# Bilinear attention and projection on one core: two engines copy, and two queues store, each finished sum of the state rows

## The chip, the core and the metric

The kernel runs on one core of a Trainium2 chip. The metric is the device time of one execution in microseconds, lower is better; before the change it is 489.55 us, the median of 3 runs (488.55 to 490.4).

## What is computed

```python
def _attn_ref(x, state):                       # x (8, 8, 512, 64), state (8, 8, 32, 64)
    scores = scale * np.matmul(x, state.transpose(0, 1, 3, 2))
    a = softmax(scores)
    xread = np.matmul(a, state)                # 512 token rows of a batch and head
    scores2 = scale * np.matmul(state, x.transpose(0, 1, 3, 2))
    a2 = softmax(scores2)
    sread = np.matmul(a2, x)                   # 32 state rows of a batch and head
    return np.concatenate([xread, sread], axis=2)

def _moe_ref(x, w1, w2, w3, w_out):            # x: (8 * 544, 512), the heads side by side
    a = x @ w1
    b = x @ w2
    h = a * b @ w3
    return h @ w_out                           # (8 * 544, 512)
```

(`softmax` stands for the four lines that subtract the maximum, take exp and divide by the sum.) The last step is, for each row, `((x w1) * (x w2)) @ (w3 w_out)`. The output has, for each of 8 batches, 512 token rows and behind them 32 state rows, each of 512 float32 numbers (2 KB).

## The kernel before

Weights are converted first, and `w3 w_out` is multiplied out once into `wo` (a high and a low part of each number). The token rows of the 8 batches follow, batch by batch. The read-outs of the state rows of all batches are collected in `sread`, and only when the last batch is done does `state_rows` (L741) turn them into output rows: 8 batches of 32 state rows are 256 rows, `n = B * NS`. It is the last part of the program, and nothing comes behind it.

`state_rows` first makes, for each of 8 blocks `ft` of 128 hidden columns, the product of the two projections, a high and a low part (`gs`). Then it makes the output rows in two groups `tt` of 128 rows (L766): group 0 holds the state rows of batches 0 to 3, group 1 those of batches 4 to 7. A group is one call of `stage2` (L362). It takes a bank of PSUM (`bank`, one of two buffers of 128 x 512 float32, tile `ps_o`), adds up 8 x 3 matmuls of 512 columns in it (`project`, L355), and calls `store` (L368). There ScalarE copies the 512 columns from PSUM into a tile `tmp` in SBUF in one instruction (L371), and four transfers (L373) write 32 rows each, one for each batch:

```python
for (dest, first, n), queue in zip(dests, cycle((nc.scalar, nc.sync))):
    queue.dma_start(out=dest, in_=o[first:first + n])
```

So the transfers go in turn to ScalarE's queue and to SyncE's queue, two on each, 64 KB each: 32 rows of 2 KB that lie one behind the other in SBUF's partitions and in the output.

The order of TensorE's and SyncE's instructions is that of the program text; ScalarE's and VectorE's is set by a scheduler, which a `high_priority` block moves ahead of other ready work. The waits between engines are put in by the framework, from the tiles that instructions read and write.

The token rows of batches 1 to 7 are stored in another way, which the prediction uses for comparison: `stored_quarter` (L497, transfers at L500) writes 128 rows of 256 columns in one transfer from ScalarE's queue, 128 KB in runs of 1 KB.

Of the kernel before, what the change touches and what calls it, by code (L numbers as in the profile page):

```python
# [22 lines left out]
F32 = mybir.dt.float32  # L23
# [6 lines left out]
P = 128  # L30
NF = 512
# [9 lines left out]
def attn_bilinear_kernel(  # L41
# [10 lines left out]
    nc = tc.nc  # L52
    B, _, NT, H, D = x_s.shape
    S = NT * P
    NP = H // 2
    NS = st.shape[3]
    KT = H * NS // P
    FT, DO = w34_k.shape[0], out.shape[2]
# [3 lines left out]
    PER = P // NS  # L62
# [6 lines left out]
    main = ctx.enter_context(tc.tile_pool(name="main", bufs=2))  # L69
# [20 lines left out]
    def bank():  # L90
        return ps_o.tile([P, NF], F32, name="ps_o")

    def two_banks():
        return ps_2.tile([P, 2, NF], F32, name="ps_2")

    def split(hi, lo, src):

        return (
            nc.scalar.copy(out=hi, in_=src),  # L99
            nc.vector.tensor_tensor(out=lo, in0=src, in1=hi.bitcast(F32), op=ALU.subtract),  # L100
        )
# [227 lines left out]
    def new_g(ft):  # L329
        if ft < FT - 2:  # L330
            return [main.tile([P, NF], F32R, name=f"g_{part}", bufs=FT - 2) for part in ("hi", "lo")]
        both = main.tile([P, 2, NF], F32R, name="g_x", bufs=2)
        return [both[:, 0], both[:, 1]]
# [21 lines left out]
    def project(ps, gs, tt, ft):  # L355
        g_hi, g_lo = (g[:, tt * P:(tt + 1) * P] for g in gs[ft])
        for k, (g, w) in enumerate(((g_hi, "lo"), (g_hi, "hi"), (g_lo, "hi"))):
            nc.tensor.matmul(  # L358
                ps[:, :DO], g, wo[w][:, ft, :], start=(ft == 0 and k == 0), stop=(ft == FT - 1 and k == 2)
            )  # L360

    def stage2(gs, tt, dests):  # L362
        ps = bank()
        for ft in range(FT):
            project(ps, gs, tt, ft)
        store(ps, dests)

    def store(ps, dests):  # L368
        o = main.tile([P, NF], F32, name="tmp", bufs=4)[:, :DO]
        with tc.high_priority():  # L370
            stored[:] = [nc.scalar.copy(out=o, in_=ps[:, :DO])]  # L371
        for (dest, first, n), queue in zip(dests, cycle((nc.scalar, nc.sync))):
            queue.dma_start(out=dest, in_=o[first:first + n])  # L373
# [20 lines left out]
    HT, HO = S // 2, DO // 2  # L394
# [253 lines left out]
    gs, acc, early = [], [], range(2)  # L648
# [92 lines left out]
    def state_rows():  # L741
        n = B * NS

        sr = att.tile([P, NP, 2, n], F32R, name="x_d", bufs=1)
        split(sr[:, :, 1], sr[:, :, 0], sread)
        gs = []
        for ft in range(FT):
            quarter, c = divmod(ft * P, NQ)
            ps = two_banks()
            for i in range(2):  # L750
                wh, wl = (main.tile([P, NP * P], F32R, name=f"sw_{part}", bufs=2 * HALF) for part in ("hi", "lo"))
                as_w = lambda t: t.rearrange("p (j f) -> p j f", j=NP)
                split(as_w(wh), as_w(wl), w_sb[:, quarter, i, :, c:c + P])
                rows = [slice(kt * P, (kt + 1) * P) for kt in range(NP)]
                for kt, ks in enumerate(rows):
                    nc.tensor.matmul(ps[:, i], wh[:, ks], sr[:, kt], start=(kt == 0), stop=False)  # L756
                for kt, ks in enumerate(rows):
                    nc.tensor.matmul(ps[:, i, :n], wl[:, ks], sr[:, kt, 1], start=False, stop=(kt == NP - 1))  # L758
            sums = main.tile([P, 2, n], F32, name="tmp", bufs=4)
            halves = ps.rearrange("p i (half n) -> p i half n", n=n)  # L760
            nc.scalar.copy(out=sums, in_=halves[:, :, 1])
            nc.vector.tensor_tensor(out=sums, in0=sums, in1=halves[:, :, 0], op=ALU.add)
            nc.vector.tensor_tensor(out=sums[:, 0], in0=sums[:, 0], in1=sums[:, 1], op=ALU.mult)
            gs.append([g[:, :n] for g in new_g(ft)])
            split(*gs[-1], sums[:, 0])
        for tt in range(n // P):  # L766
            stage2(gs, tt, [(out[tt * PER + q, S:], q * NS, NS) for q in range(PER)])


    for b in range(PLAIN, B):  # L770
# [1 line left out]
    with tc.issue_after(last_split[0].ins), tc.issue_after(last_split[1].ins):  # L772
        state_rows()
# [44 lines left out]
```

## Time and profile before

| what | value |
|---|---|
| runs | 488.55, 489.55, 490.4 us, median 489.55 |
| span of the profiled execution, first to last instruction | 486.2 us |
| time of the profiled execution outside its span | not recorded; the median is 3.35 us above the span |
| TensorE busy (matmuls) | 479.5 us, 99% of the span |
| VectorE, ScalarE busy | 393.4 us (81%), 237.6 us (49%) |
| granted TensorE clock | 1.000 of full speed, the mean of the core |
| stores of the state rows and of batch 0's token rows | 12 transfers at L373 |

The span is the time from the first to the last instruction that the profiler saw. A share of the span is an average over all stages. What happens at the very end of the program is read from the timeline, where an instruction stands with its start and its duration, and from the table of DMA windows, where the mean busy share of the core's 16 DMA engines stands with the rate that they moved. The time from a transfer's issue to its landing is counted from the start of the issuing instruction to the last of its completions.

### The profile page before, as it was taken

Reading aid. Unit: us, or ns where it says so; the run is one execution under the profiler, and the core shown is the slowest. Engines: PE = TensorE matmul, PEld = TensorE weight load, DVE = VectorE, ACT = ScalarE, POOL = GpSimd, SP = SyncE. Lnnn points to the kernel's source line nnn. Section 1 sums busy time; section 2 is a strip of 40 time slices with the busy share of each in tenths; the row PEclk is TensorE's granted clock in tenths of the full one; section 3 lists DMA queues with packets and bytes.
Section 4 is the critical chain, followed back from the end, with each engine's and each line's share of the span. In section 5 each row is a group of like instructions: output and inputs, shape, how many; then the busy total and the mean of one; then the engine's idle time right before and its main releaser. Section 6 shows DMA issues by size and latency. Waiting matters only on the chain.

```text
span 486.2 us, 8627 instructions
## 1 busy us (share of the span) xinstructions
PE 479.5 (99%) x3398; PEld 370.2 (76%) x3398; DVE 393.4 (81%) x580; ACT 237.6 (49%) x368; POOL 0.2 (0%) x4
## 2 busy tenths in 40 slices
PE   8999999999999999999999999999999999999996
PEld 5554467768788878887797779777977797899885
DVE  5778999798899589959985998599859985678870
ACT  4876984453547045605560555055515642353640
POOL 0000000000000000000000000000000000000000
PEclk9999999999999999999999999999999999999999
DMA  8996971163014404130413042304230223001101
GB/s 345 367 399 222 388 278 26 19 216 89 14 38 173 106 4 182 38 93 4 182 41 92 5 181 45 87 5 181 47 84 6 89 47 85 5 2 45 45 1 43
DMA packets 56361, 52.49 MB, mean 108 GB/s; under 512 B 42752, under 2 KB 50944, under 8 KB 51712
## 3 DMA queue, kind: packets, MB, share of 16 engines
q1 hardware_dynamic: 47488, 43.27, 26.8%
q10 hardware_dynamic: 8832, 8.65, 5.2%
q8 instruction: 27, 0.44, 0.4%
q14 instruction: 14, 0.11, 0.1%
HBM read 38.27 MB, written 8.91 MB: 97 GB/s over the span
## 4 chain that ended last, share of the span: by engine, by line
PE 93%; DVE 4%; ACT 1%; DMA 1%; issue 0%; DVEq 0%; ACTq 0%
PE ps L344 36%; PE ps_o L460 11%; PE ps L472 8%; PE ps L151 8%; PE ps_o L358 7%; PE ps_o L465 6%; PE ps L477 4%; PE ps L756 3%; PE ps_o L615 2%; PE ps L615 2%; PE ps_o L635 2%; PE ps L758 2%; PE ps_o L276 1%; DVE w_sb L138 1%; DMA raw<-in_w_k_dram 1%; PE ps L612 1%
## 5 line engine op out<-in xcount | busy, mean ns | idle before, releaser
L344 PE MATMUL ps<-at_lo,sw_hi 128*128 128x512 f32 x256 | 101.1, 395 | 0.0
L344 PE MATMUL ps<-at_hi,sw_hi 128*128 128x512 f32 x256 | 99.7, 389 | 0.0
L344 PE MATMUL ps<-at_hi,sw_lo 128*128 128x512 f32 x256 | 99.7, 389 | 0.0
L549 ACT COPY tmp<-ps 128x512 f32<-128x512 f32 x56 | 32.8, 585 | 121.5 <-PE ps L344 119.3
L344 PEld LDWEIGHTS ps<-at_lo,sw_hi 128*128 128x128 f32 x256 | 48.1, 188 | 15.9 <-DVE g_lo L100 4.2
L344 PEld LDWEIGHTS ps<-at_hi,sw_lo 128*128 128x128 f32 x256 | 48.1, 188 | 10.3
L344 PEld LDWEIGHTS ps<-at_hi,sw_hi 128*128 128x128 f32 x256 | 48.1, 188 | 9.5 <-issue 0.2
L488 DVE TENSOR_TENSOR tmp<-tmp,ps 128x512 f32<-128x512 f32 x42 | 28.9, 688 | 19.0 <-PE ps L477 18.1
L429 DVE TENSOR_TENSOR g_x<-tmp,ps 128x512 f32<-128x512 f32 x28 | 19.0, 679 | 26.4 <-ACT tmp L549 26.3
L100 DVE TENSOR_TENSOR sw_lo<-ps,sw_hi 128x1024 fp32r<-128x1024 f32 (+1 forms) x34 | 38.2, 1149 | 1.3 <-ACT sw_hi L99 1.3
L99 ACT CAST g_hi<-raw 128x512 fp32r<-128x512 f32 x42 | 24.6, 619 | 29.1 <-DVE raw L429 21.6
L151 PE MATMUL ps<-w_sb,st 64*32 64x512 f32 (+1 forms) x544 | 31.6, 570 | 0.4 <-DVE sw_lo L100 0.4
L99 ACT CAST sw_hi<-ps 128x1024 fp32r<-128x1024 f32 (+1 forms) x34 | 31.1, 969 | 1.8 <-PE ps L151 1.7
L460 PEld LDWEIGHTS ps_o<-t,g_hi 128*128 128x128 f32 x224 | 27.8, 191 | 5.0 <-issue 5.0
L99 ACT CAST g_hi<-g_x 128x512 fp32r<-128x512 f32 x42 | 25.6, 625 | 10.3 <-DVE g_x L429 5.3
L460 PE MATMUL ps_o<-t,g_hi 128*128 128x256 f32 x224 | 29.7, 286 | 0.0
L100 DVE TENSOR_TENSOR g_lo<-raw,g_hi 128x512 fp32r<-128x512 f32 x42 | 28.0, 681 | 1.6 <-PE ps_o L465 1.6
L460 PE MATMUL ps_o<-wo,g_hi 128*128 128x256 f32 x224 | 29.1, 283 | 0.0
L460 PEld LDWEIGHTS ps_o<-wo,g_hi 128*128 128x128 f32 x224 | 28.3, 192 | 0.5
L100 DVE TENSOR_TENSOR g_lo<-g_x,g_hi 128x512 fp32r<-128x512 f32 x42 | 27.2, 684 | 1.8 <-PE ps_o L465 1.8
L472 PE MATMUL ps<-t,g_hi 128*128 128x512 f32 x112 | 28.0, 392 | 0.0
L472 PEld LDWEIGHTS ps<-t,g_hi 128*128 128x128 f32 x112 | 20.2, 189 | 3.6
(125 smaller groups left out, 802.6 us busy)
## 6 DMA issues: line engine op xcount, KB each, us to landing
raw<-in_w_k_dram SPq DMA_DIRECT2D x8, 1024.0 KB, 6.0
x_d<-in_x_d_dram SPq DMA_DIRECT2D x8, 1024.0 KB, 7.4
raw<-in_w_dram SPq DMA_DIRECT2D x8, 1024.0 KB, 6.6
x_s<-in_x_s_dram SPq DMA_DIRECT2D x8, 1024.0 KB, 5.1
out_dram<-tmp ACTq DMA_DIRECT2D x56, 128.0 KB, 1.8
raw<-in_w3t_dram SPq DMA_DIRECT2D x4, 1024.0 KB, 7.0
e<-work SPq DMA_DIRECT2D x112, 32.0 KB, 2.0
sread<-turned SPq DMA_DIRECT2D x128, 4.0 KB, 1.7
```

Source lines behind the costliest of these rows:

```text
L99: nc.scalar.copy(out=hi, in_=src),
L100: nc.vector.tensor_tensor(out=lo, in0=src, in1=hi.bitcast(F32), op=ALU.subtract),
L151: nc.tensor.matmul(ps[j * NS:(j + 1) * NS, q], sts[b][rows, j], moving(rows, j), start=True, stop=True)
L344: nc.tensor.matmul(ps[:, i], w[:, kt, c:c + P], a[:, kt], start=(k == 0), stop=(k == 3 * KT - 1))
L358: nc.tensor.matmul(ps[:, :DO], g, wo[w][:, ft, :], start=(ft == 0 and k == 0), stop=(ft == FT - 1 and k == 2))
L460: nc.tensor.matmul(ps[:, tt * HO:(tt + 1) * HO], g, w(part, k), start=(fresh and k == 0 and tt == 0 and part == "lo"), stop=False, skip_gr ...
L465: nc.tensor.matmul(ps[:, tt * HO:(tt + 1) * HO], g, w("hi", k), start=False, stop=(k == QF - 1), skip_group_check=True)
L472: nc.tensor.matmul(ps[:, tt].rearrange("p (n d) -> p n d", n=2), g, w(k), start=(k == 0), stop=False, skip_group_check=True,)
L477: nc.tensor.matmul(ps[:, tt, :HO], g, w(k)[:, 0], start=False, stop=(k == QF - 1), skip_group_check=True)
L488: sum2 = lambda out, x, y: nc.vector.tensor_tensor(out=out, in0=x, in1=y, op=ALU.add)
L549: copied = nc.scalar.copy(out=a_sb, in_=ps[:, 0])
L615: nc.tensor.matmul(w34_ps[i][:, :DO], chunks[k][:, DO + i * P:DO + (i + 1) * P], w_out[k], start=(k == 0), stop=(k == FT - 1),)
```

## The change

The two calls of `stage2` in `state_rows` are written out in place. Each group's sum is now copied out of PSUM by two instructions, the first 256 columns by ScalarE and the last 256 by VectorE (`HO` is 256), and each half is stored by one transfer of 128 rows by 256 columns (128 KB): ScalarE's half on ScalarE's queue, VectorE's half on SyncE's queue. The destination is the 4 batches' slices of the output at once, 4 x 32 rows. All other calls of `store` stay.

```diff
         for tt in range(n // P):
-            stage2(gs, tt, [(out[tt * PER + q, S:], q * NS, NS) for q in range(PER)])
+            dest = out[tt * PER:(tt + 1) * PER, S:]
+            ps = bank()
+            for ft in range(FT):
+                project(ps, gs, tt, ft)
+            o = main.tile([P, NF], F32, name="tmp", bufs=4)
+            for k, (copy, queue) in enumerate(((nc.scalar.copy, nc.scalar), (nc.vector.tensor_copy, nc.sync))):
+                cols = slice(k * HO, (k + 1) * HO)
+                with tc.high_priority():
+                    copy(out=o[:, cols], in_=ps[:, cols])
+                queue.dma_start(out=dest[:, :, cols], in_=o[:, cols])
```

How the built program's instructions stand now, with the engines that each waits for in brackets (a name such as `PE_49` is the semaphore that TensorE counts up when an instruction ends). TensorE's instructions are the same as before. On ScalarE, at the end of the program (`-` before, `+` now; `tmp` is the tile in SBUF, `ps_o` the bank of PSUM, sizes are those of what is written):

```order
 L761 COPY tmp<-ps_4850 128x512 [waits PE_49,Activation_49]
 L99 CAST g_x<-tmp 128x256 [waits DVE_49]
-L371 COPY tmp<-ps_o 128x512 [waits PE_49,Activation_49]
-L373 DMA out_dram<-tmp 32x512 [waits Activation_49]
-L373 DMA out_dram<-tmp 32x512
-L371 COPY tmp<-ps_o 128x512 [waits PE_49]
-L373 DMA out_dram<-tmp 32x512 [waits Activation_49]
-L373 DMA out_dram<-tmp 32x512
-L814 UNCONDITIONAL_BRANCH
+L775 COPY tmp<-ps_o 128x256 [waits PE_49,Activation_49]
+L776 DMA out_dram<-tmp 4x32x256 [waits Activation_49]
+L775 COPY tmp<-ps_o 128x256 [waits PE_49]
```

ScalarE's copy still waits for TensorE and is half as wide; behind it stands one transfer instead of two, whose destination is written as 4 x 32 x 256 numbers.

On VectorE, at the end of the program:

```order
 L763 TENSOR_TENSOR tmp<-tmp 128x256 [waits DVE_49]
 L100 TENSOR_TENSOR g_x<-tmp,g_x 128x256 [waits Activation_49]
-L814 UNCONDITIONAL_BRANCH
+L775 COPY tmp<-ps_o 128x256 [waits Activation_49] x2
+L823 UNCONDITIONAL_BRANCH
```

The two new copies stand behind all other work of VectorE. Each waits for ScalarE (`Activation_49`), and not for TensorE.

On SyncE, at the end of the program:

```order
 L175 DMA sread<-turned 32x32 [waits DMAHW6_49]
 L175 DMA sread<-turned 32x32 [waits DMAHW7_49]
-L373 DMA out_dram<-tmp 32x512 [waits DMAHW1_49,Activation_49]
-L373 DMA out_dram<-tmp 32x512 [waits DMAHW3_49]
-L373 DMA out_dram<-tmp 32x512 [waits DMAHW5_49,Activation_49]
-L373 DMA out_dram<-tmp 32x512 [waits DMAHW7_49]
-L814 UNCONDITIONAL_BRANCH
+L776 DMA out_dram<-tmp 4x32x256 [waits DMAHW1_49,DVE_49]
+L776 DMA out_dram<-tmp 4x32x256 [waits DMAHW3_49,DVE_49]
```

SyncE issues two transfers where there were four, and each waits for VectorE's copy instead of ScalarE's.

## Rows read from the trace of the kernel before

**Rows 1.** The page: busy time, share of the span and number of instructions of each engine.

```profile
PE 479.5 (99%) x3398; PEld 370.2 (76%) x3398; DVE 393.4 (81%) x580; ACT 237.6 (49%) x368; POOL 0.2 (0%) x4
```

**Rows 2.** The chain of work that ended last, in order of time, from 470 us to the end: start, duration, what.

```profile
471.36 10.93 PE ps_o L358 x48
482.29 0.02 issue
482.31 0.59 ACT tmp L371
```

**Rows 3.** The timeline from 482.3 us to the end of the span: start, duration, engine (ACTq and SPq are issues of DMAs), line, what, in brackets the idle time before it and what ended it.

```profile
482.31 0.59 ACT L371 COPY tmp<-ps_o 128x512 f32<-128x512 f32 x1 [4.80 <-PE ps_o L358]
482.92 0.78 SPq L373 DMA_DIRECT2D out_dram<-tmp  x2
482.92 0.85 ACTq L373 DMA_DIRECT2D out_dram<-tmp  x2
```

**Rows 4.** DMA issues between 483.2 and 483.4 us, the last of the program: number, KB each, us from issue to landing; and the issues of L373 from 476 us on, with duration in ns (least, median, most), first and last start.

```profile
out_dram<-tmp SPq DMA_DIRECT2D x1, 64.0 KB, 1.6
out_dram<-tmp ACTq DMA_DIRECT2D x1, 64.0 KB, 1.9
...
L373 SPq DMA_DIRECT2D out_dram<-tmp x4: 314/393/421, 477.5 to 483.3; - x4
L373 ACTq DMA_DIRECT2D out_dram<-tmp x4: 374/412/444, 477.5 to 483.3; - x4
```

**Rows 5.** Windows of the last 3 us: from, to, length, busy time of PE, PEld, DVE, ACT and POOL with numbers of instructions, granted clock, mean busy share of the 16 DMA engines, GB/s.

```profile
483.40:483.60 0.20, 0.00 (x0) 0.00 (x0) 0.00 (x0) 0.00 (x0) 0.00 (x0) 1.00 0.00 0
483.60:483.80 0.20, 0.00 (x0) 0.00 (x0) 0.00 (x0) 0.00 (x0) 0.00 (x0) 1.00 0.33 82
...
484.00:484.20 0.20, 0.00 (x0) 0.00 (x0) 0.00 (x0) 0.00 (x0) 0.00 (x0) 1.00 0.79 195
...
484.60:484.80 0.20, 0.00 (x0) 0.00 (x0) 0.00 (x0) 0.00 (x0) 0.00 (x0) 1.00 0.91 215
484.80:485.00 0.20, 0.00 (x0) 0.00 (x0) 0.00 (x0) 0.00 (x0) 0.00 (x0) 1.00 0.10 21
485.00:485.20 0.20, 0.00 (x0) 0.00 (x0) 0.00 (x0) 0.00 (x0) 0.00 (x0) 1.00 0.00 0
```

**Rows 6.** Groups of instructions by line and shape, ScalarE: busy time, mean ns of one, idle time before and what ended it.

```profile
L371 ACT COPY tmp<-ps_o 128x512 f32<-128x512 f32 x6 | 3.5, 588 | 13.6 <-PE ps_o L358 13.6
...
L99 ACT CAST g_hi<-tmp 128x512 fp32r<-128x512 f32 x20 | 12.4, 618 | 3.4 <-DVE tmp L326 3.2
...
L99 ACT CAST g_hi<-tmp 128x256 fp32r<-128x256 f32 x6 | 2.4, 402 | 1.4 <-DVE tmp L763 1.4
```

**Rows 7.** The same view, VectorE: an operation on 512 columns that reads PSUM (`ps`), one on 128 columns that reads PSUM (`ps_o`), one on 256 columns in SBUF, and one with a single source in SBUF.

```profile
L762 DVE TENSOR_TENSOR tmp<-tmp,ps 128x512 f32<-128x512 f32 x8 | 5.5, 683 | 2.5 <-ACT tmp L761 2.5
...
L763 DVE TENSOR_TENSOR tmp<-tmp 128x256 f32<-128x256 f32 x8 | 3.4, 422 | 0.1
...
L281 DVE TENSOR_TENSOR scaled<-ps_o,sum 128x128 f32<-128x128 f32 x7 | 2.0, 284 | 0.0
...
L134 DVE TENSOR_SCALAR w_sb<-w_sb 128x512 int32<-128x512 int32 x2 | 0.8, 418 | 0.0
```

**Rows 8.** The timeline at 452 us: a VectorE instruction that waits for a ScalarE copy out of PSUM.

```profile
452.12 0.59 ACT L761 COPY tmp<-ps 128x512 f32<-128x512 f32 x1 [1.54 <-PE ps L758]
...
452.74 0.69 DVE L762 TENSOR_TENSOR tmp<-tmp,ps 128x512 f32<-128x512 f32 x1 [1.44 <-ACT tmp L761]
```

**Rows 9.** The transposes at L196 and the exponentials at L209, which both read the same PSUM tile `ps`, with duration in ns; and who waited for whom (us in total, times, longest).

```profile
L196 DVE STREAM_TRANSPOSE work<-ps x8: 1242/1243/1251, 39.9 to 369.0; 128x1024 f32<-128x1024 f32 x8
...
L209 ACT ACTIVATE e<-ps,m x16: 679/688/701, 42.6 to 371.0; 128x512 f32<-128x512 f32 x16
...
ACT e L209 <- DVE work L196: 7.5, 6, 1.9
```

**Rows 10.** A pair of 128 KB stores of token rows (L500, 128 rows by 256 columns each): the issues in the timeline, their times to landing, and windows with the columns of rows 5.

```profile
438.28 0.83 ACTq L500 DMA_DIRECT2D out_dram<-tmp  x2
...
out_dram<-tmp ACTq DMA_DIRECT2D x2, 128.0 KB, 1.8
...
438.30:439.10 0.80, 0.80 (x9) 0.80 (x8) 0.25 (x1) 0.00 (x0) 0.00 (x0) 1.00 0.00 0
439.10:439.30 0.20, 0.20 (x4) 0.20 (x3) 0.00 (x0) 0.10 (x1) 0.00 (x0) 1.00 0.71 256
439.30:439.50 0.20, 0.20 (x4) 0.20 (x3) 0.00 (x0) 0.20 (x1) 0.00 (x0) 1.00 1.03 359
...
439.90:440.10 0.20, 0.20 (x4) 0.20 (x3) 0.00 (x0) 0.20 (x1) 0.00 (x0) 1.00 0.63 210
440.10:440.30 0.20, 0.20 (x4) 0.20 (x3) 0.17 (x1) 0.20 (x2) 0.00 (x0) 1.00 0.00 0
```

**Rows 11.** Group 0, stored while group 1 is multiplied: its copy in the timeline, and windows from its issue to the end of the matmuls.

```profile
476.92 0.59 ACT L371 COPY tmp<-ps_o 128x512 f32<-128x512 f32 x1 [3.27 <-PE ps_o L358]
...
478.30:479.60 1.30, 1.30 (x7) 1.09 (x6) 0.00 (x0) 0.00 (x0) 0.00 (x0) 1.00 0.79 202
479.60:482.30 2.70, 2.67 (x12) 1.88 (x10) 0.00 (x0) 0.00 (x0) 0.00 (x0) 1.00 0.00 0
```

## Prediction, made before the changed kernel was run

> **What bounds the kernel now.** The page comes first: TensorE is busy 99% of the span [rows 1], so nothing that other engines do beside it counts, unless it makes TensorE wait. The chain of waits says where TensorE stops being the bound: its last run of matmuls ends at 482.29 us, and then one copy by ScalarE is on the path [rows 2]. The timeline of the end [rows 3] and the DMA views [rows 4, 5] show the rest, which I call the tail. The copy runs from 482.31 to 482.90. At 482.92 both queues begin to issue two transfers each; the second ones start at 483.3, and the last of these lands 1.9 us later, at 485.2 to 485.3. The DMA engines are idle until about 483.7, busy until about 484.9, and the landing comes 0.4 us after they fall idle. From there to the end of the span at 486.2 there are 0.9 us in which the engines close the program. So from the last matmul to the last landing there are 3.0 us, 0.6% of the time. That is all that this change can act on at the end.
>
> **The span and the runs.** The profiled execution has a span of 486.2 us; the runs have a median of 489.55 us, 3.35 us more. I make the sum for the tail of the span and add the difference to 489.55. A measurement of this kernel can tell about 0.5% from no change, 2.45 us: faster is below 487.1, slower is above 492.0.
>
> **Group 0 costs nothing.** Its copy starts at 476.92, and its transfers ran under group 1's matmuls: the DMA engines are idle again from 479.6 to 482.3 [rows 11]. The new copies stand behind all other work of VectorE, and the two groups use the two buffers of `ps_o`, so no matmul waits for them. If group 0's transfers kept the DMA engines busy for 3.2 us instead of 1.3, they would end at about 481.5, before group 1's are issued at 482.7. The cover is group 1's matmuls; without it, group 0 would cost what group 1 does. On ScalarE the copy of group 1 stands behind one transfer of group 0 instead of two, and it waits for TensorE until 482.29 anyway.
>
> **The copies of group 1.** ScalarE's copy of 512 columns takes 0.59 us. A cast of 256 columns is 216 ns shorter than one of 512 (618 against 402) [rows 6]; taken off, the half copy needs 0.38 us: from 482.31 to 482.69, and its transfer is issued at 482.71. VectorE's copy does not run at once with it. In the built program it waits for ScalarE, not for TensorE, and the only work of ScalarE that it can be waiting for is the other half's copy, out of the same bank. The trace shows the same between two other readers of one PSUM tile: the exponentials read `ps` and a small tile, and waited 7.5 us in all for transposes that read `ps` [rows 9]. So the copies go one behind the other, with 0.03 us between them, as where VectorE follows ScalarE at 452.74 [rows 8]. No row has a VectorE copy out of PSUM. By 683 ns for 512 and 284 ns for 128 columns from PSUM it would be 284 + 128 x 1.04 = 417 ns, and 422 ns is that of 256 columns with two sources in SBUF; the operation with one source needs 418 ns for 512 columns, so perhaps 0.2 to 0.3 us for 256 [rows 7]. I take 0.42 us, because the first row reads PSUM as this copy does. It ends at 483.14, and SyncE issues at 483.16. Against the second issues before, at 483.3, the last issue is only 0.15 us earlier.
>
> **The transfers of group 1.** Before, 4 x 64 KB were moved, now 2 x 128 KB, the same 256 KB. What differs is the shape. The stores of token rows are written as 128 x 256 and land 1.8 us after their issue; in their windows all 16 DMA engines are busy (a share of 1.03) at 359 GB/s, 22.4 GB/s for each, 45.6 ns for a run of 1 KB [rows 10]. The old stores had 32 rows in front and came to a share of 0.91 [rows 5]. Both counts in front divide by 16. The new destination is written as 4 x 32 x 256, with 4 in front. No row shows what the hardware makes of a 4. The bounds are these: all 16 engines share the work, as at L500, or four of them do all of it, one for each of the four slices.
>
> With 16 engines the later transfer lands 1.8 us after 483.16, at 484.96, 0.34 us before 485.3.
>
> With four engines, and the same four for both queues, each has 256 KB / 4 = 64 runs of 1 KB to move. They begin 0.82 us after the first issue, as at L500 (issued at 438.28, idle until 439.10 [rows 10]), at 483.53. SyncE's transfer comes 0.45 us later, while ScalarE's 32 runs still need 1.46 us, so the four engines don't fall idle. They need 64 x 45.6 ns = 2.92 us, until 486.45, and with 0.4 us to the landing it is 486.85: 1.55 us later than before. In this case the order of the copies no longer matters: the engines start after ScalarE's half and work without a gap.
>
> I take four. The count in front is the one thing in which these transfers differ from those at L500, which have the same rows, columns and bytes, and for ScalarE's half the same queue; the rows show full shares only where that count is a multiple of 16. This is an inference, and the weight of the other bound is below. The Trainium skill has a rule for it (DMA: Bandwidth & Descriptors, "Why a DMA increments its semaphore by 16 and not by 1"): the number of engines of a transfer is the largest number up to 16 that divides the slowest dimension of both sides, and for these queues it is the lowest-numbered ones. By it, 4 and 128 would give four engines, the same for both queues, and the sum +1.55 us; if all 16 took part, it would be -0.34 us. No run here shows the rule at work for a small count.
>
> **The sum.** Copies and issues -0.15 us, transfers +1.7 us: **+1.55 us, 489.55 + 1.55 = 491.1 us**, a span of about 487.7.
>
> **The rivals.**
> - *All 16 engines.* The DMA spreads 4 x 32 rows as it spreads 128. For it: every store in the trace has a share near 1 [rows 5, 10]. Against it: the count of 4. It gives 489.55 - 0.34 = 489.2 us.
> - *The copies really run at once, and 16 engines.* Both halves are issued at 482.71 and land 1.8 to 1.9 us later, at 484.6: -0.7 us, 488.85 us. Against it stand VectorE's wait and the rows of two readers of one tile [rows 9]. Even a tail that stored in no time at all after the copy would not reach 0.5%: 485.3 - 2.45 is 482.85, before the copy of today ends.
> - *Four engines that are slower than at L500.* Here the place is each of the four engines, where the runs of two queues meet. In the tail the two queues also overlapped, and at 484.0 the engines made 195 GB/s at a share of 0.79 [rows 5]: 15.4 GB/s for a busy engine, 66.4 ns for 1 KB. Then 64 runs need 4.25 us, until 487.78, the landing is at 488.18: +2.9 us, 492.4 us, slower by 0.6%. It decides from 60 ns a run on, for then 64 runs need 3.82 us and the loss is 2.45. Against it: later in the same tail the share was 0.91 at 215 GB/s, so the rate of 195 is partly one of engines that had just begun.
>
> **How the numbers follow.** Four engines at L500's rate: 0.62. All 16 engines with the copies in turn: 0.22. Copies at once with 16 engines: 0.03. Four slow engines: 0.13. The last alone is slower by over 0.5%; the runs scatter by 0.9 us to each side of the median, and 0.02 of the first case is put on that side for it: slower 0.15. No case is faster by over 0.5%, and 0.01 is left for scatter. Within 0.5%: 0.84. The likeliest time is 491.1 us, by itself with 490.2 to 492.0 by the scatter. The range of 8 in 10 reaches down to the cases with 16 engines and up to the slow four: 488.7 to 492.5 us.
>
> **What would show it.** In the profile after, the matmuls should end at about 482.3 and the half copy on ScalarE take 0.38 us. VectorE's copy should start some 0.03 us behind ScalarE's end and take 0.3 to 0.42 us. Right about the transfers: in the windows behind the last matmul the DMA share stands near 0.25, at about 90 GB/s, for some 2.9 us, and issue to landing is 3 us or more. A share near 1 for 0.8 us, with landings after 1.8 us, would make the four engines wrong and give 489.2. If VectorE's copy starts with ScalarE's, the wait was misread. A share of 0.25 at 60 GB/s would be the slow case. If the span before 482 moves by over 1 us, something else changed that I don't see.

## The result, and the profile after

The changed kernel takes 491.87 us (median of 6 runs, 490.85 to 492.74), the one before 489.53 us (median of 6, 488.55 to 490.4). The ratio is 1.0055, with a 95% interval of 1.0039 to 1.0072: slower, by about what a measurement of this kernel can tell. The forecast was 491.1 us in a range of 488.7 to 492.5, for the case that four DMA engines do all of the last store. The profile shows that case, with a tail somewhat longer than forecast.

By *tail* I mean here the time from the end of the last matmul to the end of the span. Before, it was 486.2 - 482.29 = 3.9 us [rows 2]. After, the page and the chain of waits from 470 us on (start, duration, what) say:

```profile
span 489.6 us, 8624 instructions
...
PE 480.0 (98%) x3398; PEld 370.4 (76%) x3398; DVE 394.2 (81%) x582; ACT 237.2 (48%) x368; POOL 0.2 (0%) x4
```

```profile
472.52 10.93 PE ps_o L358 x48
483.45 0.02 issue
483.47 0.38 ACT tmp L775
483.85 0.02 issue
483.87 0.42 DVE tmp L775
```

The last run of matmuls has the same 48 instructions and the same 10.93 us as in [rows 2], and ends at 483.45. The tail is 489.6 - 483.45 = 6.2 us, 2.3 us more than before. (Spans are printed rounded to 0.1 us; tails are worked out from the unrounded spans, here 489.63 and 486.17, so the last digit can differ by one.) The chain now has two copies in a row where it had one. The timeline of the tail, to set beside [rows 3]:

```profile
483.47 0.37 ACT L775 COPY tmp<-ps_o 128x256 f32<-128x256 f32 x1 [5.01 <-PE ps_o L358]
483.87 0.55 ACTq L776 DMA_DIRECT2D out_dram<-tmp  x1
483.87 0.42 DVE L775 COPY tmp<-ps_o 128x256 f32<-128x256 f32 x1 [4.96 <-ACT tmp L775]
484.32 0.58 SPq L776 DMA_DIRECT2D out_dram<-tmp  x1
```

VectorE's idle time is ended by ScalarE's copy (`<-ACT tmp L775`), so the two do not run at once; yet SyncE's only transfer is issued 0.87 us behind the matmuls, where the last issues before were 1.0 us behind them [rows 2, 4]. Up to here nothing is lost. The loss is in the windows behind it (columns as in [rows 5]: the last three are the clock, the mean share of 16 DMA engines and GB/s):

```profile
483.40:485.00 1.60, 0.03 (x1) 0.00 (x0) 0.42 (x1) 0.37 (x1) 0.00 (x0) 1.00 0.00 0
485.00:485.20 0.20, 0.00 (x0) 0.00 (x0) 0.00 (x0) 0.00 (x0) 0.00 (x0) 1.00 0.16 31
485.20:486.00 0.80, 0.00 (x0) 0.00 (x0) 0.00 (x0) 0.00 (x0) 0.00 (x0) 1.00 0.23 52
486.00:487.00 1.00, 0.00 (x0) 0.00 (x0) 0.00 (x0) 0.00 (x0) 0.00 (x0) 0.80 0.27 96
487.00:488.00 1.00, 0.00 (x0) 0.00 (x0) 0.00 (x0) 0.00 (x0) 0.00 (x0) 0.50 0.27 97
488.00:488.40 0.40, 0.00 (x0) 0.00 (x0) 0.00 (x0) 0.00 (x0) 0.00 (x0) 0.50 0.15 51
488.40:489.60 1.20, 0.00 (x0) 0.00 (x0) 0.00 (x0) 0.00 (x0) 0.00 (x0) 0.50 0.00 0
```

The share stays at about a quarter, as much as four engines of 16, for more than 3 us; before, the engines were busy for 1.2 us, with shares such as 0.79 and 0.91 [rows 5]. Two queues with a transfer each do not make it 0.5. The DMA view by queue shows why, here from 485 to 486.8 and from 487 to 488.4 us (packets, MB, share; q10 is ScalarE's queue, the only one with packets while the stores of [rows 10] run, and q1 is SyncE's):

```profile
q10 hardware_dynamic: 122, 0.12, 23.9%
...
q1 hardware_dynamic: 119, 0.12, 23.8%
```

Each stretch has packets of one queue alone. SyncE's transfer, issued at 484.32, moves none of its 1 KB runs until about 486.85, when ScalarE's is done: both need the same four engines. (The view does not name the engines. That they are four, and not 16 a quarter busy, is read from this waiting and from the shares of the experiments below.) And nothing comes at all until 485.0, 1.2 us behind the first issue. The clock falls to 0.50, the lower of its two levels, in a stretch in which TensorE has no matmul left; the stores do not slow down with it (96 and 97 GB/s). (The view of DMA issues gives no time to landing for these transfers.)

That the matmuls end 1.16 us later in this profile than in that of before is not the change: the shift is there when the last run of matmuls starts (472.52 against 471.36), before the first changed instruction, the copy of group 0 at about 478. In the experiments below, alike up to that place but for the order in which three of them read `sread`, the end of the matmuls lies anywhere from 482.56 to 484.42. I compare tails, therefore, and quote ratios of whole runs beside them. (One execution of an experiment took 801.92 us, at a mean granted TensorE clock of 0.56; neither its time nor its profile is used.)

### The profile page after: what moved, and what is told of

Its sections match the earlier page's. It is cut to its first block, busy times and chain, and to the rows that moved or that the text cites. A ratio compares the mean times of both kernels' runs of the same rounds, so it can differ in the third digit from the quotient of the medians.

```text
span 489.6 us, 8624 instructions
## 1 busy us (share of the span) xinstructions
PE 480.0 (98%) x3398; PEld 370.4 (76%) x3398; DVE 394.2 (81%) x582; ACT 237.2 (48%) x368; POOL 0.2 (0%) x4
## 4 chain that ended last, share of the span: by engine, by line
PE 78%; DVE 9%; DMA 6%; ACT 3%; SPq 2%; issue 1%; DVEq 0%; ACTq 0%
PE ps L344 31%; PE ps_o L460 11%; PE ps L472 8%; PE ps L151 6%; PE ps_o L465 5%; PE ps_o L358 5%; PE ps L477 4%; DMA raw<-in_w_k_dram 4%; PE ps L756 3%; DVE w_sb L138 2%; SPq L175 2%; DMA raw<-in_w3t_dram 2%; PE ps L758 2%; PE ps_o L276 1%; ACT ulps L130 1%; ACT w_sb L120 1%
```

## The experiments

Each kernel is the changed one with one thing altered, and with two in the runs of 8 in front and of 16 in front with one copy, as their texts say. All ratios are to the kernel before, from runs on the same chip.

**16 in front, two copies.** The rows of `sread` are taken in another order, so that a group is 16 state rows x 8 batches:

```diff
-        split(sr[:, :, 1], sr[:, :, 0], sread)
+        turned_rows = lambda t: t.rearrange("p j (s b) -> p j s b", b=B)
+        split(turned_rows(sr[:, :, 1]), turned_rows(sr[:, :, 0]), sread.rearrange("p j (b s) -> p j s b", b=B))
...
-            dest = out[tt * PER:(tt + 1) * PER, S:]
+            rows = P // B
+            dest = out[:, S + tt * rows:S + (tt + 1) * rows].rearrange("b s d -> s b d")
```

> Edit: the state rows are put in another order inside the kernel (row of the state first, batch second, by reading sread in that order when it is split), so that a group's destination is 16 x 8 x 256 instead of 4 x 32 x 256. The copies, the queues, the 128 KB and the runs of 1 KB stay those of the change. Tail means the time from the end of the last matmul to the end of the span: 3.9 us before the change, 6.1 us with it. Theory 'engines' (the count in front sets how many DMA engines work, four with the change): all 16 work, the DMA share goes near 1, landing 1.8 to 1.9 us after the issue, tail 3.6 to 3.9 us, ratio to before 0.999 to 1.000. Theory 'copies' (the two copies in turn are what costs): nothing that it names is changed, tail about 6.1 us, ratio 1.004 to 1.006. Theory 'pattern' (1 KB runs in a pattern of three dimensions are slow, whatever the count): tail about 6.1 us, same ratio.

Measured: 1.0006 (0.9993 to 1.0020). The matmuls end at 482.75, the span at 486.9: tail 4.1 us. Windows of the tail:

```profile
482.70:484.40 1.70, 0.04 (x1) 0.00 (x0) 0.42 (x1) 0.37 (x1) 0.00 (x0) 1.00 0.00 0
484.40:484.60 0.20, 0.00 (x0) 0.00 (x0) 0.00 (x0) 0.00 (x0) 0.00 (x0) 1.00 0.69 174
484.60:484.80 0.20, 0.00 (x0) 0.00 (x0) 0.00 (x0) 0.00 (x0) 0.00 (x0) 1.00 0.91 246
484.80:485.00 0.20, 0.00 (x0) 0.00 (x0) 0.00 (x0) 0.00 (x0) 0.00 (x0) 1.00 1.01 323
...
485.40:485.60 0.20, 0.00 (x0) 0.00 (x0) 0.00 (x0) 0.00 (x0) 0.00 (x0) 1.00 0.20 62
```

```profile
483.17 0.56 ACTq L778 DMA_DIRECT2D out_dram<-tmp  x1
483.18 0.42 DVE L777 COPY tmp<-ps_o 128x256 f32<-128x256 f32 x1 [4.96 <-ACT tmp L777]
483.63 0.58 SPq L778 DMA_DIRECT2D out_dram<-tmp  x1
```

```profile
out_dram<-tmp ACTq DMA_DIRECT2D x1, 128.0 KB, 2.3
out_dram<-tmp SPq DMA_DIRECT2D x1, 128.0 KB, 2.3
```

With the same copies, bytes, runs and queues, and 16 in front, the share goes to 1 and 2.1 of the 2.3 us are gone. 'Copies' and 'pattern' both expected a tail of 6.1 us. What my expectation missed is that the tail did not come below that of before: the transfers start as late as with 4 in front, 1.2 us behind the issue (483.17 to about 484.4), and land after 2.3 us, not 1.8 to 1.9.

**The transfers alone: one copy of 512 columns, the 4 x 32 x 256 transfers.**

```diff
-                with tc.high_priority():
-                    copy(out=o[:, cols], in_=ps[:, cols])
...
+            with tc.high_priority():
+                nc.scalar.copy(out=o, in_=ps)
```

> Edit: the transfers of the change alone. ScalarE copies all 512 columns in one instruction, as before; the two 4 x 32 x 256 transfers on two queues stay. Theories 'engines' and 'pattern': the copy takes 0.59 instead of 0.37 us, both transfers are issued 0.22 us later than ScalarE's is now, the four engines begin that much later, tail 6.3 us, ratio to before 1.004 to 1.007. Theory 'copies': VectorE's wait is gone, tail back to about 3.9 us, ratio 1.000.

Measured: 1.0061 (1.0046 to 1.0076), tail 490.0 - 483.55 = 6.4 us. The whole loss is there without VectorE. In its chain the copy is ScalarE's alone:

```profile
472.63 10.93 PE ps_o L358 x48
483.55 0.02 issue
483.58 0.58 ACT tmp L773
```

**The copies alone: two copies, the old four transfers**, which wait for both halves:

```diff
-                queue.dma_start(out=dest[:, :, cols], in_=o[:, cols])
+            for q in range(PER):
+                queue = (nc.scalar, nc.sync)[q % 2]
+                queue.dma_start(out=dest[q], in_=o[q * NS:(q + 1) * NS])
```

> Edit: the copies of the change alone. ScalarE and VectorE copy a half each; the four transfers of 32 rows by 512 columns before the change stay, and wait for both halves. Theories 'engines' and 'pattern': the last copy ends 0.37 + 0.02 + 0.42 = 0.81 us after the matmuls instead of 0.59, the rest is as before, tail 4.1 us, ratio 1.000 to 1.001. Theory 'copies': the cost of the change is here, tail about 6.1 us, ratio 1.004 to 1.006.

Measured: 1.0012 (0.9999 to 1.0024), tail 487.7 - 483.54 = 4.1 us. The timeline shows the 0.2 us: the issues come at 484.41, 0.87 us behind the matmuls instead of 0.63.

```profile
483.55 0.37 ACT L775 COPY tmp<-ps_o 128x256 f32<-128x256 f32 x1 [5.01 <-PE ps_o L358]
483.96 0.42 DVE L775 COPY tmp<-ps_o 128x256 f32<-128x256 f32 x1 [4.96 <-ACT tmp L775]
484.41 0.78 SPq L778 DMA_DIRECT2D out_dram<-tmp  x2
484.41 0.85 ACTq L778 DMA_DIRECT2D out_dram<-tmp  x2
```

These two runs part the theories: 'copies' expected the loss here and not there, and it fell the other way round.

**2 in front: each half stored by two transfers of 2 x 32 x 256.**

```diff
-                queue.dma_start(out=dest[:, :, cols], in_=o[:, cols])
+                for q in range(0, PER, 2):
+                    queue.dma_start(out=dest[q:q + 2, :, cols], in_=o[q * NS:(q + 2) * NS, cols])
```

> Edit: as the change, but each half is stored by two transfers of 2 x 32 x 256, so the count in front is 2. The bytes, the 1 KB runs and the copies stay; two issues more. Theory 'engines': two engines move 128 runs of 1 KB each at the 42 to 46 ns of the trace, 5.4 to 5.9 us instead of 2.7 to 2.9; DMA share near 0.125 at 45 to 48 GB/s; tail about 8.8 to 9.1 us, ratio 1.010 to 1.012. Theory 'pattern': the same runs in the same kind of pattern, tail 6.1 to 6.5 us, ratio 1.004 to 1.007. Theory 'copies': 6.1 to 6.5 us as well.

Measured: 1.0122 (1.0105 to 1.0139), tail 493.4 - 483.34 = 10.0 us. Windows:

```profile
483.30:484.90 1.60, 0.02 (x1) 0.00 (x0) 0.42 (x1) 0.37 (x1) 0.00 (x0) 1.00 0.14 47
484.90:486.00 1.10, 0.00 (x0) 0.00 (x0) 0.00 (x0) 0.00 (x0) 0.00 (x0) 1.00 0.13 47
...
490.00:492.00 2.00, 0.00 (x0) 0.00 (x0) 0.00 (x0) 0.00 (x0) 0.00 (x0) 0.50 0.13 48
```

Two engines: a share of 0.13 at 47 GB/s, as expected. The tail is 1 us longer than expected, and the first window tells why: the engines are busy before group 1 is issued at all. Group 0's transfers now take longer than the matmuls that cover them, and group 1's queue behind them. It is the cover that the prediction named, used up.

**8 in front: the order of the first experiment, each half stored by two transfers of 8 x 8 x 256.**

```diff
+                for q in range(2):
+                    queue.dma_start(out=dest[q * 8:(q + 1) * 8, :, cols], in_=o[q * 64:(q + 1) * 64, cols])
```

> Edit: the order of the state rows with the state row first, and each half stored by two transfers of 8 x 8 x 256: as the run with 2 in front, but with 8. Theory 'engines': eight engines move 32 runs of 1 KB each, 1.4 us; the last of the transfers is issued about 1.4 us behind the matmuls and lands at 3.5 to 3.7, tail 4.4 to 4.7 us; DMA share near 0.5 while they run; ratio 1.001 to 1.002. So the order of the tails by count in front is 16: 4.1, 8: 4.5, 4: 6.2, 2: 10.0 us. Theory 'pattern': no such order, tail 6.2 us.

Measured: 1.0023 (1.0011 to 1.0034), tail 487.2 - 482.56 = 4.6 us, with the share at a half:

```profile
484.40:485.00 0.60, 0.00 (x0) 0.00 (x0) 0.00 (x0) 0.00 (x0) 0.00 (x0) 1.00 0.49 137
485.00:485.60 0.60, 0.00 (x0) 0.00 (x0) 0.00 (x0) 0.00 (x0) 0.00 (x0) 1.00 0.55 184
```

So the share is 0.13, 0.25, 0.5 and 1 for 2, 4, 8 and 16 in front, and the tails are 10.0, 6.2, 4.6 and 4.1 us. (With 2 and 8 in front each half has two transfers, and the tail of 10.0 holds the rest of group 0.)

**32 in front, two dimensions: each half stored by four transfers of 32 x 256.**

```diff
+                for q in range(PER):
+                    queue.dma_start(out=dest[q, :, cols], in_=o[q * NS:(q + 1) * NS, cols])
```

> Edit: as the change, but each half is stored by four transfers of 32 x 256, one for each batch, so a pattern of two dimensions with 32 in front. Copies, bytes and 1 KB runs as in the change; six issues more per group. Theory 'engines': all 16 engines, DMA share well above 0.25; first packet 0.8 us behind the issue, not 1.2; each issue takes about 0.36 to 0.4 us, so VectorE's half is issued from 0.88 to 2.0 us behind the matmuls and lands at 3.8, tail 4.6 to 4.8 us, ratio 1.001 to 1.002. If the runs of 1 KB were what is slow: tail about 6.2 us, ratio 1.004 to 1.006.

Measured: 1.0033 (1.0020 to 1.0045), tail 489.0 - 484.42 = 4.6 us. Timeline and windows:

```profile
484.85 1.74 ACTq L777 DMA_DIRECT2D out_dram<-tmp  x4
...
485.30 1.73 SPq L777 DMA_DIRECT2D out_dram<-tmp  x4
```

```profile
484.40:485.60 1.20, 0.01 (x1) 0.00 (x0) 0.42 (x1) 0.37 (x1) 0.00 (x0) 1.00 0.00 0
485.60:486.00 0.40, 0.00 (x0) 0.00 (x0) 0.00 (x0) 0.00 (x0) 0.00 (x0) 1.00 0.30 82
486.00:487.00 1.00, 0.00 (x0) 0.00 (x0) 0.00 (x0) 0.00 (x0) 0.00 (x0) 1.00 0.48 131
```

Runs of 1 KB are not what is slow. Nor are the addresses: these transfers write the same ones as the change, so the gain of the run with 16 in front does not come from its other order of rows. Here the issuing sets the pace: 1.74 us for four, and the share is a half because the engines wait for work. The first data come about 0.8 us behind the first issue, as at L500 [rows 10], not 1.2. The ratio is higher than the tail explains (0.7 us is 0.14%); I have no reason for the rest and leave it open.

**The change in group 0 alone.**

```diff
+            if tt:
+                stage2(gs, tt, [(out[tt * PER + q, S:], q * NS, NS) for q in range(PER)])
+                continue
```

> Edit: the change for group 0 alone; group 1 is copied and stored as before the change. Prediction's step 'group 0 costs nothing': its four-engine transfers are done about 0.1 us before the last matmul ends, so the tail is that of before, 3.9 us, ratio 0.999 to 1.001. If group 0's transfers delay those of group 1 or the matmuls: tail above 4.1 us.

Measured: 1.0009 (0.9997 to 1.0022), tail 488.5 - 484.42 = 4.1 us, no difference that the runs can tell. So the loss is group 1's. In the profile of the change itself, group 0's transfers are over 0.45 us before the last matmuls are:

```profile
480.40:483.00 2.60, 2.60 (x13) 2.17 (x12) 0.00 (x0) 0.00 (x0) 0.00 (x0) 1.00 0.26 93
483.00:483.45 0.45, 0.43 (x2) 0.01 (x1) 0.00 (x0) 0.00 (x0) 0.00 (x0) 1.00 0.00 0
```

**16 in front, one copy.** The version that the runs pointed to, the first and the second experiment put together.

> Edit: the order of the state rows with 16 in front (16 x 8 x 256 transfers, one on each queue), but one ScalarE copy of 512 columns instead of two copies in turn. It is the version that the runs so far point to. Theory 'engines': all 16 engines work, and both transfers are issued at 0.63 us behind the matmuls instead of at 0.42 and 0.88; the later one lands 0.1 to 0.2 us earlier than with two copies, tail 3.9 to 4.05 us (before 3.9, two copies 4.1), ratio to before 0.999 to 1.001. Theory 'copies at once would help': the tail of the two copies should be shorter, not longer, so this one 4.1 us or more. A pattern of three dimensions is expected to keep its longer start, 1.2 us from issue to the first packet instead of 0.8.

Measured: 1.0012 (0.9999 to 1.0025). The kernel was run once more for its profile.

> The same kernel as the run of this name without b, taken again, since the profile of that one was of an execution whose TensorE clock stood at 0.56. Theory 'engines': tail 3.9 to 4.05 us, ratio to before 0.999 to 1.002; issue to first packet 1.2 us; DMA share near 1 while the transfers run. With the ratio of the first run (1.0012) no gain over before is expected.

Measured again: 1.0015 (0.9999 to 1.0030), tail 487.0 - 482.63 = 4.3 us, no better than with two copies (4.1), and no better than before (3.9). I had expected it 0.1 to 0.2 us shorter. Timeline, issues and windows of the DMA engines say what I missed:

```profile
483.26 0.58 SPq L778 DMA_DIRECT2D out_dram<-tmp  x1
483.27 0.56 ACTq L778 DMA_DIRECT2D out_dram<-tmp  x1
```

```profile
out_dram<-tmp SPq DMA_DIRECT2D x1, 128.0 KB, 2.6
out_dram<-tmp ACTq DMA_DIRECT2D x1, 128.0 KB, 2.3
```

```profile
484.40:484.60 0.20, 0.00 (x0) 0.00 (x0) 0.00 (x0) 0.00 (x0) 0.00 (x0) 1.00 0.29 77
484.60:484.80 0.20, 0.00 (x0) 0.00 (x0) 0.00 (x0) 0.00 (x0) 0.00 (x0) 1.00 0.85 210
```

Both are issued within 0.01 us, but SyncE's lands 0.3 us behind ScalarE's: two transfers that are issued together don't start together. By the DMA view, all 71 packets from 484.40 to 484.85 are of ScalarE's queue, and from 485.10 to 485.60 all but 7 of 120 are of SyncE's. Issued 0.46 us apart, as with the two copies in turn, each took 2.3 us. So the wait between the two copies costs nothing with 16 engines either, and one copy of 512 columns only lets the first transfer start 0.2 us later (issued 0.64 instead of 0.42 us behind the matmuls).

No version beat the kernel before.

## Why the prediction was right, and where its sizes were off

- **Where the loss is.** Predicted: in the tail alone, group 0 free. Shown by the run with group 0 alone (1.0009) and by the transfers alone (1.0061).
- **Four engines.** Predicted from the 4 in front, at a weight of 0.62, as an inference. Shown: the shares of 0.13, 0.25, 0.5 and 1 for 2, 4, 8 and 16. The rule that was cited from the Trainium skill (DMA: Bandwidth & Descriptors) agrees with the trace at all four counts; no run here has a count other than a power of two. The Trainium skill also says, on the same page ("Issuing engines are not separate DMA queues"), that transfers run on the same 16 DMA engines and interleave, whichever engine issued them. The trace agrees on the engines (with two queues the share stayed at 0.25), but in the change the transfers did not interleave: SyncE's came behind ScalarE's. The rival of all 16 engines falls.
- **The copies in turn.** VectorE waited for ScalarE in every run with two copies; the copies took 0.37 and 0.42 us (predicted 0.38 and 0.42), and the issues came 0.42 and 0.87 us behind the matmuls (predicted 0.42 and 0.87). The Trainium skill has a reason for such a wait (PSUM — Partial Sum Buffer, "PSUM bank collisions raise a hardware error"): two engines must not access one bank within the same partitions at the same time. No run here shows what would happen without it; that wasn't tried.
- **The order of the copies does not matter with four engines.** One copy instead of two made the tail 0.2 us longer (6.4 against 6.2), by ScalarE's later end, as the terms say.
- **The sum.** Predicted +1.55 us for the tail, measured +2.3. Two terms were too small. The data were to begin 0.82 us behind the first issue, as at L500; they began 1.2 us behind it, with 4, 8 and 16 in front alike, but 0.8 us in the run of 32 x 256. So it goes with the destination's third dimension, not with the number of engines: 0.4 us. The prediction had called the count in front the one thing in which these transfers differ from those at L500; the third dimension is another, and it was put at nothing. And 64 runs on each engine were to take 2.92 us; the windows show them from 485.0 to about 488.25, some 3.2 us. At 96 to 97 GB/s on four engines a run needs 42 ns, less than the 45.6 taken; but from 485.2 to 486.0 the four made only 52 GB/s, at a share of 0.23: they were busy and slow. Group 0's transfers began in the same way (32 GB/s at a share of 0.21 from 479.8 to 480.4). Why is open. The rest, about 0.1 us, lies between the last data and the end of the span. The 0.8 us by which the sum was short is within the scatter of 0.9 us that the forecast allowed.
- **The slow rival.** It wanted four engines at 66 ns for a run, and decided from 60. Shown: 42 ns when under way, and 50 ns over the whole stretch with its slow start (3.2 us for 64 runs). The mechanism is wrong. That its price of +2.9 us is as near to the +2.3 measured as the +1.55 of the likeliest case is due to the two short terms of that case; the time alone would not part the two, the rate does. By the ratio, 0.55%, the loss is just above the 0.5% that I had called the limit, by the medians (2.34 us) just below.
- **The case of 16 engines** was priced at -0.34 us. The run that makes it true has a tail 0.2 us longer than before. Of the 0.6 us between them 0.4 is the same late start, so its price was wrong in the main for the same reason as the forecast's.

## What to carry to other kernels

Before several transfers are put together into one, read the count that then stands in front of the pattern: with 4 there, two transfers on two queues had four of 16 DMA engines between them, and 256 KB that kept the engines busy for 1.2 us took 3.2. Such a store is free under other work (group 0) and costs in full as the last thing of the program (group 1), so look for its cover. Splitting a copy over two engines gains nothing where both halves lie in one PSUM bank and are read in turn.

## What the runs showed of the hardware that was not expected

- A store whose destination has three dimensions began 1.2 us behind its issue, and its issue took 0.55 to 0.58 us on its queue for group 1 of the change, and 0.69 and 1.14 us for group 0; with two dimensions it was 0.8 us and 0.31 to 0.44 us.
- Of two 128 KB stores that two queues issued within 0.01 us, one landed after 2.3 us and the other after 2.6; issued 0.46 us apart, both landed after 2.3.
- With four engines at work, one made 97 / 4 = 24 GB/s when under way with runs of 1 KB.
